# Another order table for the PV groups of a fused attention and FFN kernel, and a change of tiling priced at 0.104 in its planner

## The chip, the core and the metric

The kernel runs on one core of a Trainium2 chip. The metric is the device time in microseconds (us). The kernel before was run three times; its median is 1099.54 us. One further execution was taken with the hardware profiler.

## The reference

The layer has 2048 rows of 1024 numbers in bfloat16, 32 heads of 32 that share one key and one value head (multi-query attention), and a gated feed-forward part (FFN) of 3584 columns.

```python
def A(x):                                     # x: 1 x 2048 x 1024
    q = (x @ wq).reshape(B, S, 32, 32).transpose(0, 2, 1, 3)
    k, v = x @ wk, x @ wv                     # one head of 32 for all
    p = softmax(einsum("bhqd,bkd->bhqk", q, k) * 32 ** -0.5)
    o = einsum("bhqk,bkd->bhqd", p, v)
    return o.transpose(0, 2, 1, 3).reshape(B, S, 1024) @ wo

h  = x + A(layernorm(x))
h2 = h + (sigmoid(n @ w_gate) * (n @ w_up)) @ w_down     # n = layernorm(h)
```

## The kernel before

Nothing loops on the chip: a Python planner walks through the whole layer, keeps an estimated clock for each engine, and writes out every instruction of every engine in the order that it decides. What an engine issues, and when it waits on a semaphore, is fixed when the program is built.

**The work on TensorE (PE).** There are three kinds, in two tilings of the 128x128 array and a third for the scores:

- *Scores.* 512 bursts, `s_burst`. Four matmuls use the four 32-row strips of the array at once, one head each (L715, 512 columns; in the first eight groups L725, 256 columns twice). A burst fills two of three pairs of PSUM banks in `S_ps`, and ScalarE (ACT) makes two exponentials of it (L748), 128x1024 each. Burst k waits until exponential 2k - 2 is done.
- *PV groups.* 64 groups of 8 bursts, `pv_group` and `pv_wide`. Four matmuls use the four 32-column strips at once (L872; in the first groups L998 with L995). The sums of the softmax come from matmuls with ones (L911, L924; L977 in the first groups), after VectorE (DVE) has added the exponentials pairwise in `pairs` (L798, L810; L839, L848 in the first groups).
- *Fill.* All the rest: projections of q (from `zone`), the output projection `wo`, gate and up of the FFN (weights in `wgu`, `QT`, `Pr`, `zone` and `kT`), down (`zone` and `hact`). `mm` issues it either as one 128x128 matmul (L327) or, where `by_columns` says so, as four matmuls of 32 columns in the tiling of the PV groups (L329), so that no change of tiling lies between.

PV groups and fill groups share two PSUM banks, `X_ps`. `open_group` takes the bank that comes free first and makes PE wait until the group before in that bank was read out: by DVE (L886, L933, L634, L1252, L1290 and others) or, for the gate, by the tanh on ACT (L1231).

**What sets the order.** PE's clock `k_pe` advances with each item. When the exponential that the next burst waits for is due on the planner's clock, a burst of scores is issued; between bursts PE gets items of a PV group, if one is open and its exponentials are ready, or of a fill group. Each change of tiling adds `T_SW` to the clock:

```python
290            def mode(m):
291                if pe_mode[0] != m:
292                    k_pe[0] += T_SW
293                    pe_mode[0] = m
```

`PV_PLAN` has one letter for each of the 64 PV groups. It says how the group is opened: `a` and `b` after a burst of scores (with `a` not while a fill group has less than 1 us left), `c` and `e` at once behind the burst that it would otherwise follow later, with its first two items; `d` and `e` let an open PV group go on past the time at which a burst is due, up to `PV_HOLD`. A capital makes one sum of two in the first groups (`one_sum`, one L977 piece and one more L848 on DVE), and in the later groups lets the sum follow at once. The letters are read here:

```python
1567                plan = PV_PLAN[min(pv_next[0], NQC * NQ - 1)].lower()
1568                late = plan in "ce" and kk == BPG * (pv_next[0] + 1) + 1 and not busy(pv[0]) and pv_follow[0] is None
1570                hold = (busy(pv[0]) and PV_PLAN[pv_next[0] - 1] in "deDE" and pe_mode[0] == "pv" and
1571                        k_pe[0] + pv[0].left() <= due + PV_HOLD and pv[0].items[0][2]() <= k_pe[0] + 0.1)
```

DVE work that can wait stands in a list, `lo`, from which `dve_fill` takes what fits on DVE's clock before the next group has to be read out.

**Weights.** The FFN weights don't stay on the chip. 272 loads of 512 KB for gate and up go through SP's queue (`load_halves`, L243), each into a slot whose last reader on PE has finished; the down weights come once, in 14 loads on GpSimd's (POOL's) queue (`load_wd`, L243). `halves_ready` lets a fill group start when the loads have landed on the planner's clock.

Of the kernel before, what the change touches and what calls it, by code (L numbers as in the profile page):

```python
# [52 lines left out]
def when(*ticks):  # L53

    return max([0.0] + [t[0].time(t[1]) + 0.05 for t in ticks if t is not None])
# [29 lines left out]
def bass_sequential_preLN__grouped_kv_mqa__glu_gated_glu__prompt_kernel(  # L85
# [30 lines left out]
    HR = 4  # L116
    NGU = 4
    NEAR = 1
    PV_PLAN = "aaaeAcaaaaaaaacAaaabaaaAdaadaacDbaabaaaAdaabadcBcBbacaaaccabbaaa"
    WO_PLAN = "aaaaaaba"  # L120
    PV_HOLD = 1.0
    BANK_WAIT = 0.15
# [8 lines left out]
    UNIT = {t_: c_ for c_, ts_ in enumerate(UNITS) for t_ in ts_}  # L131
    LAST_G = [max(g_ for g_, x_ in enumerate(ORDER) if UNIT[x_[0]] == c_) for c_ in range(NU)]
    WD_AT, WD_GAP, WD_LATE = 6, 4, 10
    T_MM, T_FIX, T_SW, T_EXP, T_TANH, T_ADD = 0.0004167, 0.00267, 0.1, 0.91, 0.48, 0.61

    xf = A_x[0]
    of = out[0]
# [1 line left out]
    with ExitStack() as es:  # L139
# [99 lines left out]
        def _(unused):  # L239
# [55 lines left out]
            def bank_time(b):  # L295
                f = bank_free[b]
                return 1e9 if f == "open" else f(False) if callable(f) else when(f)
# [383 lines left out]
            def ring_need(k):  # L681

                r = ring(k)
                if r is None or r < 2 * BPG + 1:
                    return 0
                return r - 2 * BPG if r <= 2 * BPG + BPG else r - BPG
# [83 lines left out]
            def one_sum(g):  # L770
                return PV_PLAN[g].isupper()

# [544 lines left out]
            def busy(g):  # L1317
                return g is not None and bool(g.items)
# [231 lines left out]
            while True:  # L1550
                if not busy(pv[0]) and pv_follow[0] is not None and (
                        not busy(cur[0]) and not ffn_list or min(bank_time(b) for b in range(2)) <= k_pe[0] + 0.05 and (
                            PV_PLAN[pv_next[0] - 1].isupper() or k[0] >= NB or
                            pe_mode[0] == "s" and busy(cur[0]) and cur[0].left() > 0.9 or
# [5 lines left out]
                if wd_free and wo_val[0] and k[0] >= wd_at[0] and when(*wd_free[0][1]) <= k_pe[0]:  # L1560
# [5 lines left out]
                due = when((c_e, 2 * kk - 1))  # L1566
                plan = PV_PLAN[min(pv_next[0], NQC * NQ - 1)].lower()
                late = plan in "ce" and kk == BPG * (pv_next[0] + 1) + 1 and not busy(pv[0]) and pv_follow[0] is None
                can_s = kk < NB and pv_done[0] >= ring_need(kk - 1 if late else kk)
                hold = (busy(pv[0]) and PV_PLAN[pv_next[0] - 1] in "deDE" and pe_mode[0] == "pv" and  # L1570
                        k_pe[0] + pv[0].left() <= due + PV_HOLD and pv[0].items[0][2]() <= k_pe[0] + 0.1)
# [117 lines left out]
```

## Time and profile before

| | |
|---|---|
| three runs, median (lowest to highest) | 1099.54 us (1099.48 to 1100.16) |
| profiled execution | 1097.56 us |
| its span, from first to last instruction | 1095.7 us |
| granted TensorE clock | 0.998 |
| PE, ACT, DVE busy | 1075.8, 1007.2, 898.6 us |
| instructions | 33820 |

PE's end times are modelled in the profile and its matmuls are pipelined, so what a matmul costs is read from the start of one to the start of the next. In the timeline and the groups `x4` counts instructions; four of them with `128*32` or `32*128` run side by side. PEld is the loading of weights into the array, beside the matmuls. A name like `X_ps<-QT,wgu` says what is written and what is read. A number in square brackets is idle time of the engine before the row, with the work that ended it.

### The profile page before, as it was taken

How to read it: one execution, taken by the hardware profiler on the slowest of the kernel's cores; microseconds unless marked ns; L12 is line 12 of the kernel's file. 1: busy time of each engine (PE TensorE's matmuls, PEld its weight loads, DVE VectorE, ACT ScalarE, POOL GpSimd, SP SyncE). 2: the span in 40 equal slices, each digit the busy share in tenths (PEclk: the TensorE clock that was granted, in tenths of full speed). 3: DMA queues.
4: the chain of work that ended last, by engine and by line, in shares of the span. 5: the costliest groups of instructions: out<-in, count | busy, mean ns of one | idle time of the engine just before them, and what ended most of it. 6: DMA issues, size and time to landing. Idle time of an engine off the chain costs nothing.

```text
span 1095.7 us, 33820 instructions
## 1 busy us (share of the span) xinstructions
PE 1075.8 (98%) x14818; PEld 626.3 (57%) x14818; DVE 898.6 (82%) x1495; ACT 1007.2 (92%) x1155; POOL 65.6 (6%) x136
## 2 busy tenths in 40 slices
PE   6999999999999999999999999999999999999999
PEld 5554456654666346653666347653666446653884
DVE  7759997989988988799988889898988988889311
ACT  6999999999999999999999999999999999999110
POOL 4500110000000000000000000000000000000000
PEclk9999999999999999999999999999999999999999
DMA  9852328860977449680998519670698529891660
GB/s 218 145 125 100 107 56 243 252 152 20 253 204 203 109 107 251 195 206 20 245 243 238 121 30 275 199 173 25 161 266 230 112 58 240 218 234 39 152 174 20
DMA packets 332418, 175.84 MB, mean 160 GB/s; under 512 B 39536, under 2 KB 326512, under 8 KB 332272
## 3 DMA queue, kind: packets, MB, share of 16 engines
q1 hardware_dynamic: 326464, 163.47, 58.7%
q0 software_dynamic: 2544, 9.44, 2.7%
q8 instruction: 116, 1.90, 0.7%
q10 hardware_dynamic: 3264, 0.79, 0.4%
q14 instruction: 30, 0.25, 0.1%
HBM read 161.61 MB, written 4.19 MB: 151 GB/s over the span
## 4 chain that ended last, share of the span: by engine, by line
PE 84%; ACT 9%; DVE 3%; issue 2%; DMA 1%; POOL 1%; DVEq 0%; ACTq 0%
PE X_ps L327 47%; PE X_ps L329 13%; PE S_ps L715 12%; PE X_ps L872 8%; ACT Pr L748 7%; PE S_ps L725 1%; PE X_ps L998 1%; ACT gu L1231 1%; DMA wgu<-in_B_w_up_dram 1%; PE X_ps L911 1%; DVE st L411 1%; PE X_ps L995 1%; ACT hact L748 1%; POOL sd L390 0%; DMA zone<-zone 0%
## 5 line engine op out<-in xcount | busy, mean ns | idle before, releaser
L748 ACT ACTIVATE Pr<-S_ps 128x1024 bf16<-128x1024 f32 x992 | 943.3, 1180 | 4.1 <-PE S_ps L725 1.6
L798 DVE TENSOR_TENSOR pairs<-Pr 128x1024 bf16<-128x1024 bf16 x446 | 303.2, 682 | 27.2 <-ACT Pr L748 26.4
L810 DVE TENSOR_TENSOR pairs<-pairs 128x1024 bf16<-128x1024 bf16 x390 | 269.2, 690 | 11.9
L327 PE MATMUL X_ps<-QT,wgu 128*128 128x128 bf16 (+1 forms) x2244 | 208.2, 243 | 0.8 <-DMA wgu<-in_B_w_up_dram 0.8
L327 PEld LDWEIGHTS X_ps<-QT,wgu 128*128 128x128 bf16 x2244 | 162.9, 98 | 38.9 <-issue 26.1
L715 PE MATMUL S_ps<-QT,kT 32*128 32x512 bf16 x1792 | 176.9, 385 | 1.4 <-ACT Pr L748 1.2
L327 PE MATMUL X_ps<-QT 128*128 128x128 bf16 (+1 forms) x1636 | 151.6, 242 | 0.1
L327 PE MATMUL X_ps<-zone,hact 128*128 128x512 bf16 (+2 forms) x653 | 149.5, 371 | 0.0
L327 PEld LDWEIGHTS X_ps<-QT 128*128 128x128 bf16 x1636 | 118.6, 98 | 24.7 <-issue 16.5
L1231 ACT ACTIVATE gu<-X_ps 128x512 f32<-128x512 f32 x112 | 85.9, 767 | 45.5 <-PE X_ps L327 45.5
L715 PEld LDWEIGHTS S_ps<-QT,kT 32*128 32x128 bf16 x1792 | 45.2, 91 | 132.6 <-ACT Pr L748 122.5
L1252 DVE SCALAR_TENSOR_TENSOR hact<-gu,X_ps 128x512 bf16<-128x512 f32 x112 | 76.5, 683 | 51.5 <-PE X_ps L327 49.7
L872 PE MATMUL X_ps<-Pr,V 128*32 128x512 bf16 x1792 | 115.1, 381 | 0.4
L327 PEld LDWEIGHTS X_ps<-zone,hact 128*128 128x128 bf16 x653 | 56.4, 98 | 70.4 <-issue 17.2
L872 PEld LDWEIGHTS X_ps<-Pr,V 128*32 128x32 bf16 x1792 | 41.4, 96 | 48.8 <-issue 14.0
L329 PE MATMUL X_ps<-zone,hact 128*32 128x512 bf16 x1084 | 68.5, 380 | 0.0
L327 PE MATMUL X_ps<-zone 128*128 128x128 bf16 (+3 forms) x517 | 62.5, 267 | 3.3 <-ACT QT L632 1.3
L327 PE MATMUL X_ps<-wo,QT 128*128 128x512 bf16 x237 | 58.3, 380 | 0.0
L379 POOL CAST mean<-mv 128x1 f32<-128x1 bf16 x28 | 8.6, 309 | 818.7 <-DVE mv L1123 806.4
L329 PE MATMUL X_ps<-QT,wgu 128*32 128x256 bf16 (+1 forms) x1712 | 52.1, 262 | 0.0
L327 PEld LDWEIGHTS X_ps<-zone 128*128 128x128 bf16 x517 | 33.8, 98 | 25.5 <-issue 10.0
L329 PEld LDWEIGHTS X_ps<-QT,wgu 128*32 128x32 bf16 x1712 | 39.9, 97 | 10.6 <-issue 6.1
(106 smaller groups left out, 710.8 us busy)
## 6 DMA issues: line engine op xcount, KB each, us to landing
wgu<-in_B_w_up_dram SPq DMA_DIRECT2D x81, 512.0 KB, 5.9
wgu<-in_B_w_gate_dram SPq DMA_DIRECT2D x72, 512.0 KB, 5.4
QT<-in_B_w_gate_dram SPq DMA_DIRECT2D x57, 512.0 KB, 5.8
QT<-in_B_w_up_dram SPq DMA_DIRECT2D x48, 512.0 KB, 6.2
zone<-in_B_w_down_dram POOLq DMA_DIRECT2D x14, 512.0 KB, 5.9
out_dram<-hx SPq DMA_DIRECT2D x31, 128.0 KB, 1.7
hx<-in_A_x_dram SPq DMA_DIRECT2D x15, 256.0 KB, 2.7
Pr<-in_B_w_gate_dram SPq DMA_DIRECT2D x5, 512.0 KB, 7.2
```

Source lines behind the costliest of these rows:

```text
L327: return pe.matmul(out, lhsT=lhsT, rhs=rhs, start=start, stop=stop, skip_group_check=main[0])
L329: ins = pe.matmul(out[DH * j:DH * (j + 1)], lhsT=lhsT[:, DH * j:DH * (j + 1)], rhs=rhs, start=start, stop=stop, tile_position=(0, DH * j), ...
L411: ins = dve.bn_stats(st[:, slot, c, :], x_tile(t)[:, c * 512:(c + 1) * 512])
L715: ins = pe.matmul(S_ps[:, ((2 * k + j // 2) % 3) * 2 + j % 2, :], lhsT=kT4[DH * j:DH * (j + 1), kt * P:(kt + 1) * P], rhs=QT[DH * j:DH * ( ...
L725: ins = pe.matmul(S_ps[:, bank, kt * QC:(kt + 1) * QC], lhsT=kT4[DH * j:DH * (j + 1), (2 * b + kt) * P:(2 * b + kt + 1) * P], rhs=QT[DH * ...
L748: c_e.inc(act.activation(out=p_tile(k, n % 2), in_=S_ps[:, 2 * pr:2 * pr + 2, :].rearrange("p a (b q) -> p (a b) q", q=QC), func=ACTF.Exp, ...
L798: slot_use[x] = c_dve.inc(dve.tensor_tensor(out=dst(x), in0=p_tile(k - 1, hh), in1=p_tile(k, hh), op=ALU.add), T_ADD, 0.08)
L810: slot_use[x] = slot_use[y] = c_dve.inc(dve.tensor_tensor(out=pairs[:, x, :], in0=pairs[:, x, :], in1=pairs[:, y, :], op=ALU.add), T_ADD, ...
L872: ins = pe.matmul(bank[DH * j:DH * (j + 1), :], lhsT=V[:, kt, :], rhs=p_tile(k, j // 2)[:, j % 2 * 2:j % 2 * 2 + 2, :], start=b == 0, stop ...
L911: ins = pe.matmul(bank[DH * j:DH * (j + 1), :], lhsT=ones[:], rhs=pairs[:, sum_wide[(g, j // 2)], j % 2 * 512:(j % 2 + 1) * 512], start=Tr ...
L1231: tanh_val[n] = c_act.inc(act.activation(out=slot, in_=bank, func=ACTF.Tanh, scale=0.5), T_TANH, 0.1)
L1252: gu_read[n] = c_dve.inc(dve.scalar_tensor_tensor(out=hact[:, 2 * fs[0]:2 * fs[0] + ft, r0:r0 + len(ts) * P], in0=slot.rearrange("p (a b) ...
```

## The change

Two lines of constants change: the table of letters, and the planner's price for a change of tiling.

```diff
@@ -116,7 +116,7 @@
     NGU = 4
     NEAR = 1
-    PV_PLAN = "aaaeAcaaaaaaaacAaaabaaaAdaadaacDbaabaaaAdaabadcBcBbacaaaccabbaaa"
+    PV_PLAN = "aaacabaaacadaaaAadaaaAaAdAadaaaaadbbaaaDbaaaaaaacbbaaaaDaabCbAaa"
     WO_PLAN = "aaaaaaba"
@@ -131,7 +131,7 @@
     WD_AT, WD_GAP, WD_LATE = 6, 4, 10
-    T_MM, T_FIX, T_SW, T_EXP, T_TANH, T_ADD = 0.0004167, 0.00267, 0.1, 0.91, 0.48, 0.61
+    T_MM, T_FIX, T_SW, T_EXP, T_TANH, T_ADD = 0.0004167, 0.00267, 0.104, 0.91, 0.48, 0.61
```

29 of the 64 letters differ. Because the planner's decisions hang on one clock, the order of PE differs in many places from group 3 on, as do those of DVE, ACT and SP; POOL's is the same. The number of matmuls falls from 14,818 to 14,711, since 37 fill items that went by columns in four matmuls go as one, while group 4 gets a second sum of four.

## The prediction

> **What bounds the kernel now.** I read the page first: line 1 and the granted clock.
>
> ```profile
> span 1095.7 us, 33820 instructions
> PE 1075.8 (98%) x14818; PEld 626.3 (57%) x14818; DVE 898.6 (82%) x1495; ACT 1007.2 (92%) x1155; POOL 65.6 (6%) x136
> PEclk9999999999999999999999999999999999999999
> ```
>
> TensorE (PE) is busy nearly always at full clock, but ScalarE (ACT) is at 92%. So next the windows view, cut where the two programs part (74 us; PE's instructions before it are the same) and where the last exponential ends (1013 us).
>
> ```profile
> core 0: us, PE busy (x) PEld busy (x) DVE busy (x) ACT busy (x) POOL busy (x), PEclk, DMA share, GB/s
> 0.00:74.00 74.00, 61.01 (x1072) 41.94 (x1072) 50.96 (x125) 63.06 (x77) 26.65 (x65) 0.98 0.78 169
> 74.00:1013.00 939.00, 934.19 (x12923) 522.37 (x12919) 827.76 (x1339) 935.81 (x1065) 37.65 (x68) 1.00 0.63 164
> 1013.00:1096.00 83.00, 80.60 (x839) 61.95 (x831) 19.83 (x32) 8.36 (x14) 1.29 (x3) 1.00 0.46 116
> ```
>
> In the middle 939 us PE and ACT are both full; in the last 83 us PE works alone. Time is therefore what PE issues plus the holes between. What PE pays is read from start to start in the timeline of PE.
>
> ```profile
> 503.21 0.40 PE L872 MATMUL X_ps<-Pr,V 128*32 128x512 bf16 x4
> 503.43 1.47 PE L329 MATMUL X_ps<-zone,hact 128*32 128x512 bf16 x24
> 504.83 0.40 PE L715 MATMUL S_ps<-QT,kT 32*128 32x512 bf16 x4
> 505.16 1.47 PE L327 MATMUL X_ps<-zone,hact 128*128 128x512 bf16 x6
> 506.56 0.40 PE L715 MATMUL S_ps<-QT,kT 32*128 32x512 bf16 x4
> ```
>
> Four matmuls of a quarter array run at once; call them a piece, and call a plain 128x128 matmul (L327) a piece too. One PV piece lasts 503.43 - 503.21 = 0.22 us, and going on to L329 in the same tiling costs nothing. Six L329 pieces and the change into scores last 1.40 us: 6 x 0.216, and 0.104 for the change of tiling. One score piece and the change out last 0.33: 0.216 + 0.114. Six L327 pieces and the change into scores last 1.40 as well. So a piece costs the same by columns (L329) as plain, and each change of tiling about 0.105 us, never hidden.
>
> I laid this price list (0.216, 0.109 and 0.056 us a piece for 512, 256 and 128 columns; 0.094 to 0.111 a change by its direction, the medians of all starts) over all 14,818 starts of the timeline, from the first at 1.1 us to the last at 1093 us: 949.1 us of pieces, 110.1 of 1,051 changes, 33.1 over. Of the 33.1, 17.5 lie before 74 us. Of the 15.6 behind, 5.5 are a few ns on each piece, and 10.1 stand in 65 holes of over 30 ns. These 10.1 us are all that an order of the same work can win; the view of waits names their kinds in that stretch (it counts idle from modelled ends, so it shows 4.0 us where starts show 10.1).
>
> ```profile
> PE S_ps L715 <- ACT Pr L748: 1.2, 4, 0.6
> PE X_ps L327 <- DMA wgu<-in_B_w_up_dram: 0.8, 1, 0.8
> PE X_ps L329 <- issue: 0.7, 1, 0.7
> PE X_ps L911 <- DVE olp L886: 0.4, 2, 0.3
> ```
>
> **Part by part.** *Work.* I counted the order of both programs. The pieces are the same, with one more of 256 columns (L977: plan letter A of group 4 became a, so its two sums go to PE singly: +0.11 us; in return VectorE (DVE) has one addition fewer, L848, off the path). 37 pieces go from L329 to L327, which by the rows above costs nothing.
>
> *Changes of tiling.* 1,050 instead of 1,051: 341 instead of 337 plain into scores, 329 instead of 324 back, 8 fewer L329 into scores, 5 fewer out of scores into PV or L329, the rest smaller. By direction that is -0.14 us. The new 0.104 in the planner is near what the rows show, but it issues nothing; it only moves the planner's clock, on which the order is decided. Pieces and changes together: 1059.18 us before, 1059.16 + 0.11 in the sum after, with the same last 803 matmuls. Neither table nor price buys anything but holes.
>
> *Handovers of a bank.* All plain and PV groups share two PSUM banks; a group can start only when the one before in its bank has been read out. The biggest hole:
>
> ```profile
> 642.32 0.40 PE L911 MATMUL X_ps<-pairs,ones 128*32 128x512 bf16 x4
> 642.55 0.39 PE L329 MATMUL X_ps<-zone,hact 128*32 128x512 bf16 x4
> 642.77 0.72 DVE L933 STREAM_TRANSPOSE ols<-X_ps 128x512 f32<-128x512 f32 x1 [0.33 <-PE X_ps L911]
> 643.59 0.24 PE L329 MATMUL X_ps<-QT 128*32 128x128 bf16 x4 [0.66 <-issue]
> ...
> 797.28 0.69 DVE L886 TENSOR_TENSOR olp<-X_ps,olp 128x512 f32<-128x512 f32 x1
> ...
> 798.03 0.40 PE L911 MATMUL X_ps<-pairs,ones 128*32 128x512 bf16 x4 [0.25 <-DVE olp L886]
> ```
>
> The sum piece ends at 642.32 + 0.22; DVE's transpose (0.72) starts 0.23 later, and the next group in that bank starts at 643.59: 1.05 us after the bank's last piece. PE had one piece, 0.22 us, to put between: 0.83 us are lost. The hole at 798.03 is the same behind L886 (1.0 us after the last PV piece, 0.43 lost). So about 1.0 us of other work has to lie between two groups in one bank, and the order alone tells how much does. Below 0.9 us there are 12 handovers before, from 0.22 to 0.87, and they lost 3.0 us; after there are 7: one of 0.65 and six of 0.86 to 0.88. Before, four of 0.86 or 0.87 lost 0.03 to 0.20 each, 0.11 in the mean; six such are 0.7 and the one of 0.65 another 0.35, so 1.1: **-1.9 us**. The bounds: nothing lost at the seven (-3.0), or 0.25 at each of the six (-1.1). Handovers with 0.9 to 1.6 us between go from 59 to 72; the 59 lost 1.2 us, when DVE had an addition in front: +0.3, between 0 and +1.0.
>
> *Scores that wait for the exponential.* A burst of scores (one piece) feeds two exponentials, and starts when all exponentials but the newest are done. The ACT timeline gives its pace:
>
> ```profile
> 282.37 4.00 ACT L748 ACTIVATE Pr<-S_ps 128x1024 bf16<-128x1024 f32 x4
> 285.98 0.88 ACT L1231 ACTIVATE gu<-X_ps 128x512 f32<-128x512 f32 x1
> 286.45 4.06 ACT L748 ACTIVATE Pr<-S_ps 128x1024 bf16<-128x1024 f32 x4
> ```
>
> Four exponentials take 285.98 - 282.37 = 3.61 us, 0.90 each, a tanh 0.47. Two exponentials and a tanh are 2.28, so where a tanh falls between two bursts and PE has less work than that, scores stall:
>
> ```profile
> 285.50 0.39 PE L715 MATMUL S_ps<-QT,kT 32*128 32x512 bf16 x4
> 285.83 1.74 PE L327 MATMUL X_ps<-QT,wgu 128*128 128x128 bf16 x28
> 287.83 0.40 PE L715 MATMUL S_ps<-QT,kT 32*128 32x512 bf16 x4 [0.26 <-ACT Pr L748]
> ```
>
> PE had 1.99 us here and lost 0.33. All such waits are 36 holes with 3.6 us, in the 10.1. The three worst behind a tanh (PE work 1.66, 1.99 and 2.15 us; 1.1 us lost) stand in the new order with the same work. Stretches with a tanh and under 2.2 us rise from 9 to 20; the other six lost 0.2 together, so eleven more cost 0.4. Stretches of any kind under 1.65 us fall from 11 to 8, and the shortest grows from 0.92 to 1.51: about -0.4, from the waits that came after such stretches. I take **0.0 us**; the bounds are -1.5 (more than half of what doesn't recur goes) and +1.2 (0.11 at each of the eleven).
>
> *Weights from HBM.* PE waits once; the load behind it was issued at 195.0 (view of DMAs in the 0.4 us around each issue; the POOL row is from the timeline).
>
> ```profile
> 194.44 0.72 POOL L243 DMA_DIRECT2D zone<-in_B_w_down_dram  x1 [7.85 <-PE X_ps L327]
> ```
> ```profile
> wgu<-in_B_w_up_dram SPq DMA_DIRECT2D x1, 512.0 KB, 7.7
> ```
> ```profile
> QT<-in_B_w_gate_dram SPq DMA_DIRECT2D x1, 512.0 KB, 3.8
> ```
> ```profile
> DMA to landing us min/median/max: 3.7/5.7/9.0
> ```
>
> Beside the down weights on POOL's queue it took 7.7 us; the load at 333.4, alone, took 3.8. From the matmul that freed its slot to its first use the order gives 7.03 us of PE work, and PE lost 1.01, so issue and start add 0.4. This place stands in the new order unchanged. New are two others. The 25th load now has 7.4 us, with a POOL load planned beside it: 7.7 + 0.4 - 7.4 = 0.7 lost if it lands like the 20th, none if at the median. The 64th has 4.5 us where the shortest before was 5.8: alone it needs 3.8 + 0.4, so nothing; the next load follows 0.9 us later. I take **+0.4 us**, between 0 and +4.9 (the 64th landing at 9.0).
> [...]
>
> *Sum.* -0.14 + 0.11 - 1.9 + 0.3 + 0.0 + 0.4 = **-1.2 us**. The profiled execution, 1097.56 us (span and 1.9 around it), would become 1096.3; it stands 2.0 below the median of the runs, 1099.54, which becomes **1098.3**.
>
> **The rivals.** *More falls than the order shows* (1096.7): no handover under 1.0 costs anything (-3.0 instead of -1.9) and half of the waits for exponentials that don't recur go, with no late load (-1.5, 0). For it: the order has no stretch left under 1.5 us between two bursts, where four lost 0.3 to 0.9 each. Against it: the waits at 0.86 that the trace shows. A sum of -4.5 is the floor, 1095.0; half-way from the forecast is 1096.7.
> *The 64th load comes late* (1101.9, slower). Between its slot's last reader and its first use lie 4.5 us; from a landing of 4.1 us on, each us is one of PE, for the group waits in PE's queue with scores, PV and all else behind it. Landing like the one at 195.0, 7.7, costs 3.6: -1.2 + 3.6. For it: the median of such loads is 5.7. Against: the queue has nothing else for 8 us of PE work ahead of it, as before the load that took 3.8.
> *Nothing is gained* (1100.2): the 13 more handovers of 0.9 to 1.6 us find DVE in an addition (+1.0), the tanh stretches cost their +1.2, and the holes only move: -0.14 + 0.11 - 1.9 + 1.0 + 1.2 + 0.4 = +0.7.
>
> **How the numbers follow.** Forecast 0.50, with its own range of 1096.9 to 1099.7 (the bounds of handovers, waits and loads but the 64th, added as squares); more falls 0.20; the late load 0.14; nothing gained 0.16. A difference under 0.2% (2.2 us) is about what a measurement of this kernel can tell from no change; faster by more means below 1097.34. That holds all of the first rival and a fifth of the forecast: 0.20 + 0.10 = 0.30. Slower by more is above 1101.74: a good half of the late load, 0.08, and 0.07 of the last rival, where a load is late by 2 us as well. Together 0.15; within: 0.55. The range 1095.6 to 1101.4 leaves out the end of the first rival and the later half of the late load.
>
> **What would show it.** After: PE's busy time within 1 us of 1075.8 less the holes; no idle of 0.66 before an L329 and none of 0.25 before L911; the wait for wgu near 200 us still there, and a second one some 10 us later or none; the S waits behind ACT near 1.2. A wait for wgu or QT of over 1 us near 340 us decides for the late load. Wrong altogether would be a change of over 5 us: then PE paid something other than pieces, changes and these three kinds of hole.

## The result, and the profile after

The changed kernel took 1097.89 us in the median of 12 runs (1095.28 to 1099.17), the kernel before 1099.77 us beside it (12 runs, 1097.69 to 1100.85): a ratio of 0.9983, with a 95% interval of 0.9975 to 0.9991. The forecast was 1098.3 in a range of 1095.6 to 1101.4. The same kernel was measured beside the kernel before on two later occasions (the experiments new_again and new_third): 0.9991 and 0.9996. A variant whose only difference is the time of one load on POOL was measured twice (wd_late, wd_late_two) and gave 1.0001 and 0.9986. The mean of the five is 0.9991, that is 1.0 us less. The first interval and that of wd_late don't touch, so what one occasion gives is uncertain by more than its interval; the four later ones were also on four different chips, which can't be told apart from the occasion. The five ratios have a standard deviation of 0.0007, which gives their mean a 95% interval of about 0.0009 to either side, as much as it differs from 1. A gain is likely, and its size open.

The page after, lines 1 and 2, and the windows view with the same cuts:

```profile
span 1095.8 us, 33600 instructions
PE 1077.7 (98%) x14711; PEld 627.5 (57%) x14711; DVE 897.6 (82%) x1494; ACT 1006.9 (92%) x1155; POOL 65.9 (6%) x136
PEclk9899999999999999999999999999999999999999
```
```profile
core 0: us, PE busy (x) PEld busy (x) DVE busy (x) ACT busy (x) POOL busy (x), PEclk, DMA share, GB/s
0.00:74.00 74.00, 61.39 (x1036) 42.40 (x1040) 49.87 (x123) 62.08 (x76) 26.41 (x65) 0.95 0.75 165
74.00:1013.00 939.00, 935.66 (x12855) 523.19 (x12847) 827.87 (x1341) 936.46 (x1066) 38.20 (x68) 1.00 0.63 164
1013.00:1096.00 83.00, 80.68 (x840) 61.90 (x828) 19.84 (x32) 8.36 (x14) 1.29 (x3) 1.00 0.48 116
```

PE is 1.5 us busier in the middle stretch than before, and its granted clock in the head is 0.95 instead of 0.98. The profiled execution took 1097.53 us, nearly the 1097.56 of before; in the head, where the order of PE is the same in both, it lost 1.0 us more. The price list, laid over the starts of all matmuls as in the prediction, separates the two. All figures are us; a hole is time over the price, and a handover is named by the PE work between two groups in one bank:

| | pieces and changes | over, to 74 us | over, behind 74 | of it: few ns a piece | holes over 30 ns | scores waiting | handovers under 0.9 | 0.9 to 1.6 |
|---|---|---|---|---|---|---|---|---|
| before | 1059.18 | 17.45 | 15.64 | 5.51 | 65: 10.13 | 36: 3.59 | 12: 2.97 | 59: 1.23 |
| after | 1059.16 | 18.48 | 14.72 | 5.86 | 81: 8.86 | 53: 4.34 | 7: 0.81 | 72: 1.86 |
| new_again | 1059.16 | 19.43 | 15.32 | 5.86 | 77: 9.46 | 4.08 | 7: 0.81 | 72: 1.89 |
| new_third | 1059.16 | 18.75 | 18.20 | 5.83 | 93: 12.37 | 4.32 | 7: 0.81 | 72: 1.78 |

Behind 74 us the changed order is 0.92 us shorter in this pair of traces. That is not all the order's doing: 0.58 of it are pauses before matmuls for which the program has no wait (0.57 at 75.9 and 0.23 at 473.3 us before, 0.22 at 76.6 after). Nor is it steady: five traces of this order on PE have 14.72, 15.32, 18.20, and 14.62 and 14.59 (wd_late and wd_late_two), and there is only one of before. What the table does show are the kinds of hole. The holes of 0.83 at 643.6, 0.45, 0.43, 0.33 and 0.32 at handovers are gone. The waits view of PE, from 74 to 1013 us, has two rows left; behind it the place of the first, from the timeline of PE:

```profile
PE X_ps L327 <- DMA wgu<-in_B_w_up_dram: 1.1, 1, 1.1
PE S_ps L715 <- ACT Pr L748: 0.9, 2, 0.6
```
```profile
203.34 1.36 PE L327 MATMUL X_ps<-QT,wgu 128*128 128x256 bf16 x11 [1.14 <-DMA wgu<-in_B_w_up_dram]
```

No L329 waits 0.66 any longer, and no L911 0.25; the wait for `wgu` near 200 us stands, as forecast.

### The profile page after: what moved, and what is told of

The parts are those of the page before. It is cut to its first block, busy times and chain, and to the rows that moved or that the text cites. A ratio compares the mean times of both kernels' runs of the same rounds, so it can differ in the third digit from the quotient of the medians.

```text
span 1095.8 us, 33600 instructions
## 1 busy us (share of the span) xinstructions
PE 1077.7 (98%) x14711; PEld 627.5 (57%) x14711; DVE 897.6 (82%) x1494; ACT 1006.9 (92%) x1155; POOL 65.9 (6%) x136
## 5 line engine op out<-in xcount | busy, mean ns | idle before, releaser
L327 PE MATMUL X_ps<-QT,wgu 128*128 128x128 bf16 (+1 forms) x2242 | 207.9, 243 | 1.1 <-DMA wgu<-in_B_w_up_dram 1.1
L327 PEld LDWEIGHTS X_ps<-QT,wgu 128*128 128x128 bf16 x2242 | 162.5, 98 | 38.8 <-issue 26.8
L327 PE MATMUL X_ps<-zone,hact 128*128 128x512 bf16 (+2 forms) x686 | 157.5, 372 | 0.0
L327 PE MATMUL X_ps<-QT 128*128 128x128 bf16 (+1 forms) x1652 | 153.0, 242 | 0.1
L327 PEld LDWEIGHTS X_ps<-QT 128*128 128x128 bf16 x1652 | 119.8, 98 | 25.7 <-issue 15.6
L1252 DVE SCALAR_TENSOR_TENSOR hact<-gu,X_ps 128x512 bf16<-128x512 f32 x112 | 76.6, 684 | 48.4 <-PE X_ps L327 47.3
L327 PEld LDWEIGHTS X_ps<-zone,hact 128*128 128x128 bf16 x686 | 59.1, 98 | 73.9 <-issue 18.5
L327 PE MATMUL X_ps<-zone 128*128 128x128 bf16 (+3 forms) x513 | 62.4, 270 | 2.8 <-ACT QT L632 1.3
L329 PE MATMUL X_ps<-zone,hact 128*32 128x512 bf16 x952 | 61.3, 380 | 0.0
L327 PE MATMUL X_ps<-wo,QT 128*128 128x512 bf16 x232 | 57.1, 381 | 0.0
L329 PE MATMUL X_ps<-QT,wgu 128*32 128x256 bf16 (+1 forms) x1720 | 52.6, 262 | 0.0
L327 PEld LDWEIGHTS X_ps<-zone 128*128 128x128 bf16 x513 | 35.0, 101 | 24.6 <-issue 9.3
L329 PEld LDWEIGHTS X_ps<-QT,wgu 128*32 128x32 bf16 x1720 | 40.4, 97 | 11.5 <-issue 6.8
```

The costliest lines, as they stand in the source:

```text
L327: return pe.matmul(out, lhsT=lhsT, rhs=rhs, start=start, stop=stop, skip_group_check=main[0])
L329: ins = pe.matmul(out[DH * j:DH * (j + 1)], lhsT=lhsT[:, DH * j:DH * (j + 1)], rhs=rhs, start=start, stop=stop, tile_position=(0, DH * j), ...
L1252: gu_read[n] = c_dve.inc(dve.scalar_tensor_tensor(out=hact[:, 2 * fs[0]:2 * fs[0] + ft, r0:r0 + len(ts) * P], in0=slot.rearrange("p (a b) ...
```

## The experiments

Each kernel was timed beside the kernel before on the same chip. Holes and handovers are counted as in the table above.

**Which of the two constants?** The old table with the new price, and the new table with the old price.

```diff
 old_table_new_price (kernel before)
-    T_MM, T_FIX, T_SW, T_EXP, T_TANH, T_ADD = 0.0004167, 0.00267, 0.1, 0.91, 0.48, 0.61
+    T_MM, T_FIX, T_SW, T_EXP, T_TANH, T_ADD = 0.0004167, 0.00267, 0.104, 0.91, 0.48, 0.61
 new_table_old_price (kernel after)
-    T_MM, T_FIX, T_SW, T_EXP, T_TANH, T_ADD = 0.0004167, 0.00267, 0.104, 0.91, 0.48, 0.61
+    T_MM, T_FIX, T_SW, T_EXP, T_TANH, T_ADD = 0.0004167, 0.00267, 0.1, 0.91, 0.48, 0.61
```

> The old table with the new price 0.104. If what changes the time is the order, and a table fits only the clock that it was chosen on: the pieces cost the same (priced 1059.21 us against 1059.18), but 25 handovers of a bank have under 0.9 us of work between (12 before, 7 after), with 10.6 us missing to 1.0 us each (3.7 before, of which 3.0 were lost); so about 8.2 are lost instead of 3.0, and the time is 5.5 us over before, between +2.5 and +8. If the new price is what brings the gain (the planner's clock nearer to the chip's), it is 1 to 2 us under before, as the full change is.

> The new table with the old price 0.1. By the order: priced 1057.38 us, 1.8 less than before; 25 handovers under 0.9 us with 9.6 us missing, so 7.5 lost instead of 3.0; together +3 us over before, between 0 and +6. If the table is what brings the gain and the price is an accident, 1 to 2 us under before. If neither matters and the gain is a difference between executions, within 0.5 us of before.

Measured: 1117.37 us for the old table with the new price (4 runs; 1.0160 of before, 1.0139 to 1.0181) and 1109.16 for the new table with the old price (4 runs; 1.0092, 1.0077 to 1.0107). The direction is as expected, the size over three times as large (+18 and +10 us where +5.5 and +3 were forecast), above the range of each. Pieces and changes stay at 1059.21 and 1057.38; handovers under 0.9 us rise to 26 and 25 and lose 13.2 and 9.2, and scores wait 8.0 and 8.2 (3.59 before). Three of the rows of PE's waits in the old table with the new price:

```profile
PE S_ps L715 <- ACT Pr L748: 4.9, 7, 1.4
...
PE X_ps L329 <- DVE QT L634: 1.4, 1, 1.4
PE X_ps L329 <- DVE ols L933: 1.3, 3, 0.7
```

The expectation had 8.2 and 7.5 for the handovers and nothing for the scores. Among the scores are bursts back to back, where the planner had neither a fill group nor a PV item ready. The timeline of PE in the same kernel:

```profile
422.70 0.40 PE L715 MATMUL S_ps<-QT,kT 32*128 32x512 bf16 x4 [0.44 <-ACT Pr L748]
424.53 0.40 PE L715 MATMUL S_ps<-QT,kT 32*128 32x512 bf16 x4 [1.44 <-ACT Pr L748]
```

In the old table with the new price, five pauses of 0.5 to 1.0 us ahead of matmuls that wait for nothing (about 4 together, 0.8 in all before) and a stretch of half clock near 294 us come on top; their cause stays open.

So neither constant brings the gain by itself: each table is good with its own price alone, and 4 ns a change, over a thousand changes, unfit it.

**Do handovers bind PE?** First the other way round: DVE reads the sum bank of each of 28 groups twice.

```diff
-                    need(dve, tick, ols_read[g - 2 if g > NQ + 1 else NQ - 1])
+                    need(dve, tick, ols_read[g - 2 if g > NQ + 1 else NQ - 1]); c_dve.wait(dve, c_dve.inc(dve.transpose(ols[:], bank))[1])
```

> The new kernel, with the same orders on all engines but that DVE reads each of the 28 sum groups of the later PV groups out of PSUM twice (the transpose of 0.72 us, done once more ahead of the real one). If a handover of a bank binds as told, the next group in that bank can start 1.05 + 0.72 us after the sum's end; with what lies between in the new trace 8.7 us are missing on 22 of the 28, so the time is 9 us over the new kernel (1107), between +6 and +13, since DVE's other work also comes 0.7 us later each time. If DVE has slack there and PE is bound by its own work alone, it stays within 1 us of the new kernel.

Measured: 1106.04 us (4 runs; 1.0061 of before, 1.0044 to 1.0078). That is within the forecast of +6 to +13 us over the changed kernel (8.2 over its first median, 1097.89; 6.8 over before beside it). Its trace has 8.1 us more behind 74 us than the changed kernel, and the handovers of 0.9 to 1.6 us lose about 10 instead of 1.86 (some of PE's records are missing in this trace). One of them, in the timelines of PE and DVE:

```profile
588.02 0.40 PE L911 MATMUL X_ps<-pairs,ones 128*32 128x512 bf16 x4
588.24 1.16 PE L329 MATMUL X_ps<-QT 128*32 128x256 bf16 x36
589.99 0.24 PE L329 MATMUL X_ps<-QT,wgu 128*32 128x128 bf16 x4 [0.59 <-DVE ols L933]
```
```profile
588.47 0.72 DVE L932 STREAM_TRANSPOSE ols<-X_ps 128x512 f32<-128x512 f32 x1
589.22 0.72 DVE L933 STREAM_TRANSPOSE ols<-X_ps 128x512 f32<-128x512 f32 x1
```

The 36 L329 matmuls (nine pieces of 0.109, 0.98 us) had been cover enough for one reading and are not for two: PE starts 0.05 us after the second ends at 589.94. DVE was busy only 18 us longer (915.6 against 897.6 on the page).

Then less of it: two of the readings take half of the columns, in both kernels. The planner's prices stay, so PE's order does too.

```diff
-                    olp_val[0] = c_dve.inc(dve.tensor_tensor(out=olp[:], in0=bank, in1=olp[:], op=ALU.add), 0.62, 0.08)
+                    olp_val[0] = c_dve.inc(dve.tensor_tensor(out=olp[:, 0:256], in0=bank[:, 0:256], in1=olp[:, 0:256], op=ALU.add), 0.62, 0.08)
...
-                    free = c_dve.inc(dve.transpose(ols[:], bank), 0.75, 0.08)
+                    free = c_dve.inc(dve.transpose(ols[:, 0:256], bank[:, 0:256]), 0.75, 0.08)
```

> The kernel before, in which two readings of a PV bank on DVE (L886 and L933, some 28 of each) take 256 of the 512 columns; the planner's prices, and so the order of PE, stay as they were. What is left out is half of the second PV sum and half of the softmax sums of the later groups. In the profile of before five handovers behind these two readings lost 0.83 (at 643.6 us), 0.43, 0.33, 0.32 and 0.14: 2.05 us together. If the handover price is what the new table saved, a reading that is some 0.33 shorter leaves 0.5 of the 0.83 and 0.1 of the 0.43 and nothing of the others: -1.4 us, with what a freer DVE gives on top (0 to -1). So 0.9986 of before at the profile's holes, 1.4 to 2.4 us less. Theory 2 (the holes are only slack against ACT, DVE and the loads, which comes back elsewhere): less than 0.7 us is gained.

> The same two shorter readings in the changed kernel. Only two handovers behind them are short there (0.08 and 0.10 lost). If the table's gain lies in the handovers, there is little left to win: -0.2 us, and up to -1 from a freer DVE; the distance to the kernel before with the same readings shrinks from 0.92 us behind 74 us to between 0 and -0.5 (the new table then stands equal or a little behind, for its other terms are +0.75 and +0.63). Theory 2: both kernels gain alike and the distance stays near 1 us.

Measured: 1099.15 us for before with half readings (12 runs; 1.0009 of before, 0.9998 to 1.0020), 1098.94 for after (11 runs; 0.9996, 0.9987 to 1.0005). Where the handovers were short, the price came off to the hundredth: 0.83 became 0.56, 0.33 became 0.06, 0.43 became 0.16 and 0.32 became 0.05, 0.27 each. The first of them, timeline of before with half readings:

```profile
646.63 0.39 PE L329 MATMUL X_ps<-zone,hact 128*32 128x512 bf16 x4
646.85 0.45 DVE L933 STREAM_TRANSPOSE ols<-X_ps 128x256 f32<-128x256 f32 x1 [0.33 <-PE X_ps L911]
...
647.41 0.24 PE L329 MATMUL X_ps<-QT 128*32 128x128 bf16 x4 [0.39 <-issue]
```

The reading is 0.45 instead of 0.72, and the next group starts 0.27 sooner. The fifth (0.14 at 407 us) did not move; there the bank is read by the copy L883, which was left whole. But the time did not fall, where 1.4 to 2.4 us less was forecast. In the trace, the two handovers that follow within a us lost 0.31 more, scores waited 4.26 instead of 3.59, and the late weights cost 1.23 at 206 us instead of 1.01. Two pauses of 0.56 and 0.53 us (430.5 and 540.9 us) stand ahead of matmuls that wait for nothing, and nothing ties them to the readings; without them this trace would be 0.6 us shorter behind 74 us than that of before. So theory 1 (the readings are the price of a handover) holds at each place. By the runs theory 2 (what is saved comes back elsewhere) holds for the whole, but the trace shows the way back only in part.

With the halved readings the two kernels stand 0.2 us apart in the medians, and 0.04 in the trace behind 74 us (16.16 and 16.12), where it was 0.92. That is what theory 1 had said of the distance, but it doesn't carry it: by the ratios (1.0009 and 0.9996) they stand 1.4 us apart, more than the two with whole readings on the same occasion (new_third, 0.4), and both traces are of the slowest execution of their kernel, the one with the two pauses, the other with a load late by 1.14 us and 0.85 lost at 78.5. Whether the distance shrank is not shown.

**Is it what PE issues?** Two variants move PE's work and leave most else. In the first no fill item goes by columns; in the second all letters are a.

```diff
 plain_fill (kernel after, in mm)
-                if pe_mode[0] != "pv":
+                if True:
 all_a (kernel after)
-    PV_PLAN = "aaacabaaacadaaaAadaaaAaAdAadaaaaadbbaaaDbaaaaaaacbbaaaaDaabCbAaa"
+    PV_PLAN = "aaaaaaaaaaaaaaaaaaaaaaaaaaaaaaaaaaaaaaaaaaaaaaaaaaaaaaaaaaaaaaaa"
```

> The new kernel with the planner's order unchanged, but every fill matmul that went by columns (L329, 1009 pieces) issued as one 128x128 matmul (L327). That makes 115 more changes of tiling (1165 instead of 1050). By the price list: pieces the same, +10.8 us of changes, less 0.5 to 1 us of holes that this fills: 9 to 11 us over the new kernel. If a piece by columns costs more than a plain one (four matmuls and four weight loads for one), the loss is smaller: with 5 ns more for each piece it would be 5 us less, 4 to 6 us; if changes of tiling were hidden, it would be faster than the new kernel.

> All 64 letters a, price 0.104. By the order: priced 1061.4 us, 2.25 over before (26 more changes of tiling, less else); 8 handovers of a bank under 0.9 us of work with 2.0 us missing to 1.0 (before 12 with 3.7), so 1.6 lost instead of 3.0; one stretch between bursts as short as 0.22 us, so one more hole of about 1.5. Together +1 to +3 us over before, which is near what 64 searched letters bring. If the letters do more than the changes and the holes that the order shows, it is slower than +5.

Measured: plain_fill 1105.05 us (4 runs; 1.0043 of before, 1.0028 to 1.0058), some 5.8 over the changed kernel of the same occasion where 9 to 11 was expected. The price list held: 115 more changes make 10.8 us, and the few ns a piece came to 6.24 against 5.86, although some four thousand matmuls of 32 columns had become a quarter as many of 128 (11,684 in all instead of 14,711). But the holes shrank from 8.9 and 9.5 (after, new_again) to 4.3: scores waited 1.7, handovers lost 0.8 in all, and the late load near 203 us cost 0.29 instead of 1.30. All waits of PE between 74 and 1013 us:

```profile
PE S_ps L715 <- ACT Pr L748: 0.7, 2, 0.5
PE X_ps L327 <- DMA wgu<-in_B_w_gate_dram: 0.5, 1, 0.5
PE X_ps L327 <- DMA QT<-in_B_w_gate_dram: 0.2, 1, 0.2
```

Of the 10.8 us of added PE work almost half came back: the waits shrank, as they would if ACT, DVE and the loads then stand further ahead. The holes are in part slack against them, not loss.

all_a took 1108.76 us (4 runs; 1.0076, 1.0062 to 1.0091), 8.5 more than before where 1 to 3 was expected. The counted terms were right: pieces and changes +2.25, handovers under 0.9 us 1.72, and the one stretch too short between two bursts, forecast at 1.5, lost 2.11. In the timeline of PE:

```profile
418.39 0.56 PE L327 MATMUL X_ps<-QT 128*128 128x128 bf16 x7
419.57 0.40 PE L715 MATMUL S_ps<-QT,kT 32*128 32x512 bf16 x4 [0.62 <-ACT Pr L748]
421.89 0.39 PE L715 MATMUL S_ps<-QT,kT 32*128 32x512 bf16 x4 [1.93 <-ACT Pr L748]
...
553.57 0.39 PE L715 MATMUL S_ps<-QT,kT 32*128 32x512 bf16 x3
555.26 0.39 PE L715 MATMUL S_ps<-QT,kT 32*128 32x512 bf16 x1 [1.30 <-issue]
```

What was not counted are five waits for DMA (3.5 us; 1.1 before) and pauses with no wait in the program (4.3; 0.8 before). The last two rows show the longest: three of a burst's four matmuls ran, and the fourth 1.69 us later, though nothing in the program lies between them. The letters are worth several us here by the time; how much of that is order, and how much such pauses, one trace can't tell.

**What moves the late weights?** On POOL one load of down weights, the ninth, was to be made later (wd_late), then the tenth as well (wd_late_two). The two kernels on record are the same, character for character, and have this edit:

```diff
                 if wd_next[0] >= NFP - WD_LATE:
                     need(pool, (c_e, 2 * k[0] - 2))
+                if wd_next[0] == 8:
+                    c_e.wait(pool, 2 * k[0] + 4)
```

> The new kernel, with one load of down weights on POOL's queue (the ninth) issued six exponentials later, about 5 us; PE, DVE, ACT and SP have the same order. If the load of up weights lands late beside it because they share the DMA engines, that load lands in about 5 us instead of 8.0, the wait for it near 203 us (1.3 us from start to start) goes, and the time is 1.0 to 1.3 us under the new kernel, about 1096.7 where the new kernel has 1097.9. If the load is slow for another reason, or the time comes back at the next wait for an exponential, the new kernel's time stays within 0.4 us.

> The changed kernel with the ninth and the tenth load of down weights on POOL's queue six exponentials later; the orders of PE, ACT, DVE and SP stay the same. In four executions of the changed order the wait for the 26th gate load (near 221 us) was 0, 0.79, 1.14 and 1.93 us, as that load landed in 6.4, 7.7, 8.0 and 8.8 us beside the tenth load on POOL; the wait near 203 us was 0.98 to 1.36. Theory (the two loads share bandwidth with POOL's): the 26th lands in under 7.0 and its wait is gone, the wait near 203 falls to 0.7, and nothing new is late by over 0.3 behind them: 0.9 to 1.5 us under the mean of the changed kernel, 1098.0 beside 1099.1 of before, 0.9985 to 0.9995. Rival (SP's own loads fill the queues there, and a POOL load only moves to the next one): another load near 225 to 235 us is late by 0.5 to 2, and the time is that of the changed kernel, 0.9983 to 1.0.

Measured: 1099.59 us (12 runs; 1.0001 of before, 0.9993 to 1.0010) and 1098.32 (11 runs; 0.9986, 0.9973 to 0.9999). So these are two measurements of one kernel, and the edit did not do what was meant. POOL's timeline, first after, then wd_late_two:

```profile
177.75 0.72 POOL L243 DMA_DIRECT2D zone<-in_B_w_down_dram  x1 [7.25 <-ACT Pr L748]
186.07 0.72 POOL L243 DMA_DIRECT2D zone<-in_B_w_down_dram  x1 [7.59 <-ACT Pr L748]
194.64 0.72 POOL L243 DMA_DIRECT2D zone<-in_B_w_down_dram  x1 [7.85 <-PE X_ps L327]
...
212.16 0.72 POOL L243 DMA_DIRECT2D zone<-in_B_w_down_dram  x1 [8.49 <-ACT Pr L748]
```
```profile
185.93 0.72 POOL L243 DMA_DIRECT2D zone<-in_B_w_down_dram  x1 [13.99 <-ACT Pr L748]
187.51 0.72 POOL L243 DMA_DIRECT2D zone<-in_B_w_down_dram  x1 [0.85 <-ACT Pr L748]
196.08 0.72 POOL L243 DMA_DIRECT2D zone<-in_B_w_down_dram  x1 [7.85 <-PE X_ps L327]
```

This execution runs 1.44 us later than that of after. Measured from there, only the first of the three loads has moved, by 6.7 us: the ninth, at 177.75 in after. The loads that POOL issues beside the two late ones are the eleventh (194.64) and the thirteenth (212.16), not the ninth and the tenth, so whether those two collide with POOL was not tried. What the runs give are two more executions of the changed order on PE, with waits of 0.71 and 0.54 us near 204 us and 0.45 and 0.32 near 220.

**The same kernel again.**

> The new kernel once more, beside the kernels of this call. Its first runs were 1.9 us under before (1097.89 against 1099.77), but its profile is only 0.9 us shorter behind 74 us, and a granted half clock of 6.8 us in the first 35 us cost it 1.0 more there than before had in its profile (3.4 us). If the order is worth what its holes say, it is 0.9 to 1.5 us under before; if 1.9 is right, the profile missed a part.

> The changed kernel once more beside before. First measurement 0.9983, second 0.9991 of before. By the holes of the trace 0.92 us, 0.9992; between 0.9982 and 0.9998 is expected. A ratio under 0.998 would say that the holes miss part of the gain.

Measured: 1099.27 us beside 1100.27 (12 and 23 runs; 0.9991, 0.9982 to 1.0000), and 1098.67 beside 1099.07 (12 and 29 runs; 0.9996, 0.9984 to 1.0007). The trace of new_third, the slowest of its twelve executions (1101.55 us), shows one reason for the spread. The timeline of PE, the row of the DMA view for the gate load that it waits for, and the windows ahead of it and behind:

```profile
219.34 0.50 PE L327 MATMUL X_ps<-QT,wgu 128*128 128x256 bf16 x3
221.61 2.00 PE L327 MATMUL X_ps<-QT,wgu 128*128 128x256 bf16 x9 [1.77 <-DMA wgu<-in_B_w_gate_dram]
```
```profile
wgu<-in_B_w_gate_dram SPq DMA_DIRECT2D x1, 512.0 KB, 8.8
```
```profile
215.00:221.60 6.60, 4.84 (x57) 3.01 (x46) 6.25 (x12) 6.60 (x9) 0.72 (x1) 1.00 0.93 284
221.60:225.00 3.40, 3.39 (x33) 1.97 (x37) 2.38 (x4) 1.27 (x2) 0.00 (x0) 0.52 0.73 212
```

This is the 26th gate or up load. It landed in 6.4, 7.2, 7.3, 7.7, 8.0 and 8.8 us in six executions of the changed order (after, wd_late_two, wd_late, new_again, after_half_read, new_third), and PE lost 0, 0.32, 0.45, 0.79, 1.14 and 1.93 for it: each us from about 7.0 on is one of PE. In new_third the clock fell to half behind the wait as well, for 3.4 us, and the pieces in that window took 1.57 us more than their price. In the one trace of before the load issued at the same time took 7.1 us and nobody waited.

**Does the clock in the head set the spread?** 73 matmuls of zeros fill PE's waits before 74 us; the order of all else is the same.

```diff
+            # called ahead of bursts 1, 3, 4, 5, 6 and 7 and of one projection, n = 5 to 18
+            def keep_busy(n):
+                g, k_ = _Group([], None), k_pe[0]
+                open_group(g)
+                bank_free[g.bank] = None
+                for i in range(n):
+                    pe.matmul(X_ps[:, g.bank, 0:P], lhsT=warm[:, 0:P], rhs=warm[:, 0:P], start=True, stop=True, skip_group_check=True)
+                k_pe[0] = k_
```

> The new kernel, with 73 matmuls of zeros (128 columns, into a free bank) added in the waits of PE between 15 and 29 us; every other instruction stands in the same order on all engines. If the spread between executions comes from the clock, which falls to half for 3.4 to 10.2 us at 25 to 28 us because PE has too little to do there, the half clock goes, the granted clock is 0.999, and the time is 1.5 to 2.5 us under the new kernel, with a smaller spread. If the clock does not hang on PE's work there, the zeros cost 0 to 1 us.

Measured: 1099.60 us (11 runs; 0.9997 of before, 0.9987 to 1.0007), where 1.5 to 2.5 less than the changed kernel was expected. Windows of new_again, then of warm_head:

```profile
25.00:30.00 5.00, 2.78 (x24) 1.32 (x24) 4.89 (x11) 3.64 (x6) 4.13 (x8) 0.50 1.04 218
30.00:40.00 10.00, 9.98 (x124) 6.71 (x120) 5.89 (x15) 8.35 (x11) 4.46 (x12) 0.75 0.81 142
```
```profile
25.00:30.00 5.00, 4.25 (x70) 3.22 (x71) 4.86 (x13) 4.69 (x7) 3.77 (x9) 1.00 0.92 185
30.00:40.00 10.00, 9.68 (x140) 6.14 (x140) 8.10 (x20) 10.00 (x13) 5.61 (x13) 1.00 1.11 175
```

The half clock is gone, and the exponentials of warm_head run 2.10 us ahead of those of new_again from 100 to 174 us (1.34 ahead of after). At 416 us the lead is 1.10, and against after it is a lag of 0.46. Where it went, in the timeline of PE in warm_head:

```profile
175.77 0.42 PE L329 MATMUL X_ps<-QT,wgu 128*32 128x256 bf16 x8 [0.59 <-issue]
203.09 1.36 PE L327 MATMUL X_ps<-QT,wgu 128*128 128x256 bf16 x11 [1.72 <-DMA wgu<-in_B_w_up_dram]
...
289.14 1.48 PE L327 MATMUL X_ps<-QT,wgu 128*128 128x256 bf16 x12 [0.42 <-DMA QT<-hn]
...
356.47 0.45 PE L327 MATMUL X_ps<-QT,wgu 128*128 128x128 bf16 x5 [0.23 <-DMA wgu<-in_B_w_up_dram]
```

An earlier PE meets the same loads: the wait near 203 us grows by 0.6 over that of after, and two that were none appear, at 289 for the rows of `hn` and at 356 for weights. The pause at 175.8 stands ahead of a matmul that waits for nothing and stays unexplained; from it to 190 us the lead over after fell by 0.64 us, of 1.80 in all. The rest was given back to the loads in this execution; that this explains the medians is likely but not shown. No variant beat the changed kernel by more than the occasions differ.

## Why the prediction was right

*Pieces and changes.* Forecast unchanged, 1059.18 to 1059.16 us; so they are. (The 0.11 of the added piece is in the 1059.16, and not to be added to it as the prediction has it; its sum counts it once.) That L329 and L327 cost the same and a change 0.094 to 0.111 us was tested by plain_fill and held.

*Short handovers, -1.9.* Measured -2.16 in the trace (2.97 to 0.81), and 0.81 in both repetitions. The price of about 1.0 us from the last piece to the next group goes with DVE's reading (0.72 of the 1.05 us at 643.59), as both experiments on it show. This is the one kind of hole that the new order has clearly less of. That it is what shortens the time is argued from the count: halving two readings took 1.06 us from such holes, and the time stayed.

*Handovers of 0.9 to 1.6, +0.3.* Measured +0.63. The term was sized by the mean loss of the 59 and has twice that: 18 gate and up groups of 256 columns lose 1.52 here, where 15 had lost 0.87.

*Scores behind exponentials, 0.0 between -1.5 and +1.2.* Measured +0.75. The two worst recur, as foreseen (0.66 at 162.6 and 0.33 at 288.4); the third cost 0.05 instead of 0.13. There are 53 holes instead of 36, nearly all small. Behind a tanh they lost 1.78 instead of 1.41 us, so the 0.4 that the prediction charged for more such stretches is about what came. What failed is the credit of 0.4 for the shortest stretches that went: the holes without a tanh lost 2.56 instead of 2.19.

*Weights, +0.4.* The sum was +0.29 in the first trace, from the 20th load alone (1.30 instead of 1.01; it landed in 8.0 us instead of 7.7). The step that failed is the place. The 25th landed in 4.7 us and had 2.4 to spare. It is the 26th, behind it on the same queue and not looked at, that the changed order needs early. It cost 0 to 1.93 us, 0.77 in the mean of six executions, and once a stretch of half clock. The prediction charged a possible 0.7 to the wrong load. Against 1.01 in the one trace of before, the two late loads cost from 0.15 less (wd_late_two) to 1.90 more (new_third, and 1.57 there for the half clock). The 64th, on which the slower rival hung, landed in 3.9 us, 0.35 before it would have cost anything, as its row in the DMA view says:

```profile
wgu<-in_B_w_up_dram SPq DMA_DIRECT2D x1, 512.0 KB, 3.9
```

In warm_head PE waited for the same load, the 0.23 us shown above at 356: the rival's mechanism is there, its size is not. The POOL load that was planned beside the 25th was issued in after at 212.16 us, 2.1 behind it and 0.2 ahead of the 26th. The 26th took 6.4 to 8.8 us beside such a load of POOL's; no run took that one away, so that POOL's load is what made it slow is not shown.

*Not counted.* The hole at 76 us fell from 0.57 to 0.22 in the first trace, and was 0.57 again in new_third: chance. So is the pause of 0.23 at 473 us that is gone: before with half readings, which has the same order on PE, doesn't have it. The few ns a piece rose by 0.35. About 0.4 less in holes of other kinds, that pause among them, is the rest.

*Sum.* -1.2 forecast, -0.92 in the first trace behind 74 us, -1.0 in the mean ratio of five occasions. The median of the first, 1.88 less, is more than the trace bears out. That the sum came so near is in part luck: the scores and the longer handovers took 0.75 and 0.33 more than forecast, the short ones gave 0.26 more, and pauses that no term had gave 0.58. That the profiled execution was 1097.53 us and not the forecast 1096.3 lies in the head, which stands 1.03 us further over the price in the same order (18.48 and 17.45), with 6.8 us of half clock instead of 3.4.

*The rivals.* More falls than the order shows: no, waits at 0.86 to 0.88 remain (0.08 to 0.20 each). Nothing is gained: its terms came half true or more (+0.63 of 1.0 and +0.75 of 1.2), and on two of the occasions (0.9996 and 1.0001) the time was close to it, so it isn't ruled out. PE's busy time rose by 1.9 where it was to stay within 1 us of 1075.8 less the holes: by 0.4 up to 74 us, where the granted clock was 0.95 instead of 0.98, and by 1.5 from there to 1013 us, where it was 1.00 in both and PE's idle time fell from 4.8 to 3.3.

## What to carry to other kernels

Take the price of each operation from start to start, lay it over the whole order, and what remains are holes that can be counted by kind; for a reordering of the same work that count gave the direction of every order tried here. Its size was up to four times too small where scores, loads or pauses came in that it didn't cover, so it has to cover stretches where nothing is ready, and every load whose slack shrinks, not only the one with the least. Loads that landed late and pauses with no wait differed from one execution to the next by as much as the change was worth (0 to 1.93 us for the 26th load, 0.03 to 0.57 for the pause at 76 us). A table of order belongs to the price in its planner: when the price changed by 4%, the same table cost 11 to 18 us more. And holes are not a sum to be collected: where PE work was added, almost half of it came back, and where holes of 1.06 us were taken away the time stayed.

## What the runs showed of the hardware

TensorE's granted clock fell to half in the head (0.50 in each us from 28 to 31 in before and from 28 to 34 in after), for 3.4 us in the profiled execution of before, 6.8 in after and 10.2 in new_again, worked out from the windows view of each as twice the missing clock times the length of a window; for new_again that is the two rows above, 2 x (0.50 x 5 + 0.25 x 10) = 10.0, and 0.2 in the window before. The over-price of the head rose with it, 17.45, 18.48, 19.43: about 1 us for each 3.4 in these three traces, and three points show no more than that. Behind a wait of 1.77 us in mid-kernel, as in new_third, one such stretch cost 1.57 us. In old_table_new_price it fell at 294 us too (0.53 in the window below, 1.00 in the 8 us before it); the windows view:

```profile
294.00:301.00 7.00, 6.06 (x49) 2.96 (x53) 5.80 (x10) 5.83 (x8) 0.00 (x0) 0.53 1.16 279
```

Ahead of the stretch in new_third stood a wait of 1.77 us, ahead of this one waits of 1.10 and 0.42. Behind a wait of 1.93 us in all_a, with 0.62 just before it, the clock stayed at 1.00 (422 to 426 us). What decides between them no run here shows.

A second thing: one 512 KB load of the same place in the same order took 6.4 to 8.8 us from one execution to the next (the 26th), while in the 64th place one took 3.9 in after. PE lost 0 to 1.93 us for the 26th, where this whole change is worth 1.0 in the mean of five ratios.

A third: PE stood still at places where the program asks for no wait, for 0.2 to 1.7 us, even within the four matmuls of one burst (all_a, 555.26). In three traces of the changed kernel it was at 76 us alone (0.22 in after, 0.03 in new_again, 0.57 in new_third); in before it was also at 473 us, and in before_half_read, with the same order on PE, at 430 and 541 instead. Why, no run here shows.
